# Flags spread over the partitions by a matmul, ranks computed later, and a last output half stored in two pieces

## Chip, cores and metric

One NeuronCore of a Trainium2 chip runs the whole program. The metric is device time in microseconds (us); three plain runs of the kernel before gave 236.74, 237.10 and 233.53 us (median 236.74). One more execution was profiled; its own time was 234.33 us, and its span, from the first to the last instruction, 232.5 us.

## What is computed

The reference is an attention followed by a two-layer network. Four batches of eight heads, 768 positions, head size 64. Each head has a flag: a flagged ("retrieval") head attends to every earlier position, the others to four sink positions and a window of 64. The attention's output, regrouped to 3072 tokens of 512, goes through `h = x @ w_in` (512 to 2048), `g = h - tanh(h)` and `g @ w_out` (2048 to 512).

```python
causal = rel >= 0
stream_keep = causal & (is_sink | in_win)
mask = np.where(is_retrieval[head], causal, stream_keep)
scores = np.where(mask, scale * (q @ k.T), -1e9)
a = softmax(scores)                       # per head
x = (a @ v).transpose(0, 2, 1, 3).reshape(4 * 768, 512)
h = x @ w_in
out = (h - np.tanh(h)) @ w_out            # float32, 3072 x 512
```

The flags are eight 64-bit integers, that is sixteen 32-bit words, in DRAM.

## The kernel before

The 3072 tokens are worked off in twelve tiles `t` of 256 tokens, three to a batch. For each tile the stages are: load q, k, v; turn them so that the head size lies on the partitions (`st_T` on TensorE for tiles 0 to 2, a transposing DMA in `turn` from tile 3 on); scores (`st_S`, line 987) and their exponential on ScalarE (line 1000); the product with v (`st_A`, line 1080), which VectorE divides by the row sums (lines 1100, 1112, 1127); x turned (`st_X`, lines 1161 and 873, for tiles 0 and 1, a transposing DMA in `st_X_tile`, line 1144, from tile 2 on); the first layer in eight units of 256 columns (`H_unit`: eight matmuls at line 1190 into `ph`, tanh on ScalarE at line 1202, the difference on VectorE at line 1209 into `gt`); and the second layer (`O_group`: matmuls at line 1248 into `po`, then `store`, lines 1222 to 1234).

All operations are recorded first (`op`, `dma`) and then put in order by `Plan.run`, which plays them through with estimated costs and writes out each engine's queue in that order. Every engine then works its queue off strictly in order, so a change of one recorded operation, its cost or its dependences can move instructions on all five engines. `Plan.run` also hands out the PSUM banks: the tag `one` has four, and `tp`, `av`, `xp`, `ph` and `po` all live in them, so TensorE has to wait for the reader of a bank before it fills it anew. Spare time of TensorE before 18 us of the planned time is filled with matmuls of `ones` (line 1392, `wm`).

The parts that matter here:

- `flags` (line 717) turns the sixteen words, which line 1308 has loaded into all 128 partitions, into one flag per head (`nz`, `rflag`) and a threshold (`thr`); `masks` (line 746) makes from it the additive masks `m4` of tiles 0 and 1, and `scale_v` multiplies v by it.
- `by_rank` (line 758) sorts the heads, flagged ones first: some fifteen small VectorE operations that end in `perm_i` (line 814), masks `m4r` and `mS` for tiles 3 and up, and two register loads of the ranks (line 863), one on GpSimd's queue, which then gathers the heads by rank (`gather`, line 560), and one on VectorE's.
- GpSimd's queue issues the loads of v for the first tiles (line 434), of q and k for tiles 1 and 2 (`t16p`, line 467), of the weights (`win`, line 539; `wout`, line 550) and of tile 3 (line 528). SyncE's queue issues the loads of tiles 4 and up (line 528), the transposing DMAs (lines 492 and 1144) and the stores (line 1234). `t16p` is copied on VectorE (line 478) before `st_T` of tiles 1 and 2.
- The last token block's output is projected in two halves of 256 columns at the end (lines 1463 and 1464): the first is copied out of PSUM by VectorE and stored by SyncE's queue, the second by ScalarE and ScalarE's queue. Each `store` takes an `ot` buffer of its own.

Of the kernel before, what the change touches and what calls it, by code (L numbers as in the profile page):

```python
# [7 lines left out]
FP32 = mybir.dt.float32  # L8
FP16 = mybir.dt.float16
I32 = mybir.dt.int32  # L10
# [6 lines left out]
class Plan:  # L17
# [24 lines left out]
    def op(self, eng, ns, fn, r=(), w=(), dma=None, prio=None, port=False):  # L42
        i = len(self.ops)
        deps = set()
        for k in r:
            if k in self.writer:
                deps.add(self.writer[k])
            if k[0] in self.PSUM:
                deps.update(j for j in self.readers.get(k, ()) if self.ops[j][0] != eng)
            self.readers.setdefault(k, []).append(i)  # L50
        for k in w:
            if k in self.writer:
                deps.add(self.writer[k])
# [12 lines left out]
        return i  # L66
# [154 lines left out]
def kernel(  # L221
# [49 lines left out]
    engs = {"ACT": nc.scalar, "DVE": nc.vector, "POOL": nc.gpsimd, "SP": nc.sync}  # L271
    Engine = mybir.EngineType

    retr_i = const.tile([128, 2 * H], I32, name="retr_i")
    ones = const.tile([128, 128], FP16, name="ones")
    warm = const.tile([128, 1], FP32, name="warm")
    ident16 = const.tile([128, 128], FP16, name="ident16")
    A4 = const.tile([128, 4, 128], FP16, name="A4")
    sinks = const.tile([128, 128], FP16, name="sinks")
    nz = const.tile([128, 2 * H], FP32, name="nz")  # L280
    rflag = const.tile([128, H], FP32, name="rflag")
    thr = const.tile([128, H], FP32, name="thr")
    m4 = const.tile([128, H, 512], FP16, name="m4")
    rflag0 = const.tile([128, H], FP32, name="rflag0")
    nzp = nz[:].rearrange("p (h two) -> p h two", two=2)
    m4r = const.tile([128, NGEN, 512], FP16, name="m4r")
    rflagr = const.tile([128, NGEN], FP32, name="rflagr")
    rflagr0 = const.tile([128, NGEN], FP32, name="rflagr0")
# [19 lines left out]
        ot=([128, DM], FP32), v1=([128, 2 * NG, H, D + 1], FP16), vf=([128, 4, H, D + 1], FP16),  # L308
    )
    many = []  # L310
    TE = (("ACT", "ACT"), ("DVE", "DVE"), ("DVE", "DVE"))
    SV = "POOL"
    FILLS = 30
    FILL_END = 18000.0
    CASTS = (("ACT", "ACT"), ("ACT", "DVE"))
    CUT = (-10.5, -6.0, 2.25, 13.5)
    GATE = {3: (1, 0), 4: (1, 1)}
    CUT1 = (-10.5, -6.0, 2.25, 13.5)
    FROM = 3
    BR = 8  # L320
    MASKS = 2
    A2 = (10, 14)
    ORDER = (0, 1, 2, 3, 4, 5, "t2", "r3", 6, 7)

    def program(first):
# [18 lines left out]
        def buf(tag):  # L344

            i = rot[tag] = rot.get(tag, -1) + 1
            box = []

            def get():
                if not box:  # L350
                    shp, dt = shape[tag]
                    at = P.bank_of[tag, i] if tag in P.BANKS else i % bufs[tag]
                    box.append(pools[tag].tile(shp, dt, tag=f"{tag}{at}", name=f"{tag}_{i}"))
                return box[0]

            return get, i
# [358 lines left out]
                select(mS[0:64, 3, :], ones[0:64, :], 0.0, n_sink_i - 1, 0, -1, "mS3")  # L715

        def flags():
            op(
                "DVE", 175,
                lambda: nc.vector.tensor_scalar(  # L720
                    out=nz[:], in0=retr_i[:], scalar1=0, scalar2=None, op0=ALU.not_equal
                ),
                r=["retr"], w=["nz"],
            )
            op(
                "DVE", 165,
                lambda: nc.vector.tensor_max(out=rflag[:], in0=nzp[:, :, 0], in1=nzp[:, :, 1]),
                r=["nz"], w=["rflag"],
            )
            op(  # L730
                "DVE", 165,
                lambda: nc.vector.tensor_scalar(
                    out=thr[:], in0=rflag[:], scalar1=-0.5, scalar2=0.75, op0=ALU.mult, op1=ALU.add
                ),
                r=["rflag"], w=["thr"],
            )
            op(
                "DVE", 165,
                lambda: nc.vector.scalar_tensor_tensor(
                    out=rflag0[:], in0=sinks[:, 0:1].to_broadcast([128, H]), scalar=0.75,  # L740
                    in1=rflag[:], op0=ALU.is_ge, op1=ALU.max,
                ),
                r=["sinks", "rflag"], w=["rflag0"],
            )
# [13 lines left out]
        def by_rank():  # L758

            def dve(ns, fn, r, w):  # L760
                op("DVE", ns, fn, r=r, w=w)

            one = iota[:].unsqueeze(1).to_broadcast([128, H, H])
            dve(
# [404 lines left out]
            )  # L1169


        gts, pos, chain = {}, {}, []
        FU = 2
        NFU = NFB // FU

# [38 lines left out]
            )  # L1214

        def store(t, ts, po, key, c0, c1, eng, ring):
            ot, io = buf("ot")
            t0 = t * TT + ts * 128

            def evac():  # L1220
                if eng == "ACT":
                    nc.scalar.activation(  # L1222
                        out=ot()[:, c0:c1], in_=po()[:, c0:c1], func=AF.Copy, scale=1.0 / XS
                    )
                else:
                    nc.vector.tensor_scalar(
                        out=ot()[:, c0:c1], in0=po()[:, c0:c1], scalar1=1.0 / XS, scalar2=None,
                        op0=ALU.mult,
                    )

            op(eng, 110 + 0.95 * (c1 - c0), evac, r=[key], w=[("ot", io), ("od",) + key])
            dma(
                ring, 420,
                lambda: engs[ring].dma_start(out=out[t0 : t0 + 128, c0:c1], in_=ot()[:, c0:c1]),
                128, (c1 - c0) * 0.18, r=[("ot", io)],
            )

        def O_group(t, ts, f0, f1, c0=0, c1=DM, eng="ACT", ring="SP"):

            if f0 == 0:  # L1240
                pos[t] = bank([128, DM], FP32, "one", f"po{t}_{ts}_{c0}")
            po, key = pos[t]
            gt, ig = gts[t]
            for fa in range(f0, f1, 2):

                def mm(fa=fa):
                    for f in range(fa, fa + 2):
                        nc.tensor.matmul(  # L1248
                            out=po()[:, c0:c1], lhsT=gt()[:, f, ts * 128 : ts * 128 + 128],
                            rhs=w_out_t[:, f, c0:c1], start=(f == 0), stop=(f == NFB - 1),  # L1250
                        )

                halves = range(c0 * 2 // DM, (c1 * 2 - 1) // DM + 1)
                if fa == 0:
                    chain.append(key)
                op(
                    "PE", 2 * 0.422 * (c1 - c0), mm,
                    r=[("wout", x, fa * 2 // NFB) for x in halves] + [("gt", ig, fa // FU)]
                    + [("od",) + c for c in chain[-3:-2] if fa == 0], w=[key],
                )  # L1260
            if f1 == NFB:
                store(t, ts, po, key, c0, c1, eng, ring)
# [42 lines left out]
        if first:  # L1305
            dma(
                "ACT", 400,
                lambda: nc.scalar.dma_start(
                    out=retr_i[:], in_=is_retrieval.bitcast(I32).partition_broadcast(128)
                ),  # L1310
                128, 20.0, w=["retr"],
            )
            load_first()
            constants()
            iq = raws[0][1]
            for half in range(2):
# [24 lines left out]
        else:  # L1341
            for t in range(3):
                load_cast(t)
            for n in range(HP):
                st_T(n, TE)
                st_S([(n, 0)])
# [114 lines left out]
            op("SP", 500, count, r=["count", ("gt", gts[last][1], NFU - 1)])  # L1461
        O_group(last, 0, 0, NFB)
        O_group(last, 1, 0, NFB, 0, half, "DVE", "SP")
        O_group(last, 1, 0, NFB, half, DM, "ACT", "ACT")

        with tc.manual_schedule():
            P.run()
# [40 lines left out]
```

## Time and profile before

| | |
|---|---|
| runs | 236.74, 237.10, 233.53 us, median 236.74 |
| profiled execution | 234.33 us, span 232.5 us |
| TensorE clock granted | 0.998 of full speed over the span |
| TensorE matmul busy | 223.0 us (96%), 2345 matmuls |
| VectorE, ScalarE, GpSimd busy | 145.2, 142.9, 100.1 us |
| DMA | 35.3 MB, mean 152 GB/s over the span |

A profile row gives start and duration in us, the engine, the line, what is written and read, and how often; in brackets the idle time of the engine just before it and what ended it. PE is TensorE's matmuls, PEld its weight loads, DVE is VectorE, ACT ScalarE, POOL GpSimd, SP SyncE; a name with q is a queue that issues. Matmuls overlap, so a row of n matmuls lasts n spacings plus the fill of the last. A transfer's landing is the moment at which its semaphore lets a waiter go on; the trace has it for each.

### The profile page before, as it was taken

The page shows a single profiled execution, that of the slowest core. Times are in us where ns is not written, and L with a number is a line of the kernel's source. Part 1 is how long each engine was busy: PE and PEld are TensorE (multiplying, and loading weights), DVE is VectorE, ACT ScalarE, POOL GpSimd, SP SyncE. Part 2 cuts the span into 40 slices and gives each one's busy share as a digit, 9 for nine tenths or more (in the row PEclk, how much of TensorE's full clock was granted, in tenths as well). Part 3 has the DMA queues.
Part 4 walks back from the last instruction along what each step waited for, and adds up shares of the span by engine and source line. Part 5 has one row for each costly group of instructions (what it writes and reads, how often), then busy time and mean ns, then how long its engine had stood idle before and what let it go on. Part 6 is the DMA issues. An engine that isn't in the chain of part 4 may idle for free. (4 is left out here: it accounts for less than half of the span.)

```text
span 232.5 us, 6139 instructions
## 1 busy us (share of the span) xinstructions
PE 223.0 (96%) x2345; PEld 159.5 (69%) x2345; DVE 145.2 (62%) x345; ACT 142.9 (61%) x223; POOL 100.1 (43%) x231
## 2 busy tenths in 40 slices
PE   7888999999999999998999999999999999999992
PEld 7546798888986767656766666667676667666652
DVE  3789668976774967777585465668674465534310
ACT  2867768976466868664855857466835946443320
POOL 8998352990283729467461959291000000000000
PEclk9999999999999999999999999999999999999999
DMA  4999999978999999979999999945103011301112
GB/s 122 195 193 206 197 199 223 209 114 212 245 208 233 163 233 168 244 171 215 187 210 227 227 185 243 230 114 119 39 30 85 15 38 45 93 12 38 45 61 81
DMA packets 103105, 35.31 MB, mean 152 GB/s; under 512 B 90784, under 2 KB 100256, under 8 KB 103072
## 3 DMA queue, kind: packets, MB, share of 16 engines
q1 hardware_dynamic: 85632, 27.14, 57.4%
q0 software_dynamic: 17152, 7.60, 25.0%
q8 instruction: 19, 0.31, 0.6%
q10 hardware_dynamic: 288, 0.14, 0.2%
q14 instruction: 14, 0.11, 0.2%
HBM read 27.27 MB, written 6.29 MB: 144 GB/s over the span
## 5 line engine op out<-in xcount | busy, mean ns | idle before, releaser
L1190 PE MATMUL ph<-xT,win 128*128 128x256 f16 x768 | 99.0, 273 | 1.0 <-DVE gt L1209 0.9
L1248 PE MATMUL po<-wout,gt 128*128 128x512 f16 (+1 forms) x464 | 97.6, 342 | 0.2 <-DVE gt L1209 0.2
L1209 DVE SCALAR_TENSOR_TENSOR gt<-th,ph 128x512 f16<-128x512 f32 x96 | 65.2, 683 | 38.8 <-ACT th L1202 38.3
L1202 ACT ACTIVATE th<-ph 128x512 f32<-128x512 f32 x96 | 57.4, 600 | 51.0 <-PE ph L1190 50.9
L1190 PEld LDWEIGHTS <-win 128*128 128x128 f16 x768 | 71.2, 98 | 18.6 <-DVE gt L1209 1.3
L1000 ACT ACTIVATE pt<-sc 128x768 f16<-128x768 f32 (+1 forms) x60 | 53.1, 918 | 13.7 <-PE sc L987 13.5
L1248 PEld LDWEIGHTS <-gt 128*128 128x128 f16 x464 | 43.1, 98 | 22.8 <-issue 0.4
L572 POOL CAST t<-rawqk 128x256 f16 x72 | 29.1, 451 | 36.5 <-DMA rawqk<-in_k_dram 23.5
L1112 DVE TENSOR_TENSOR x16t<-av,rinv 128x128 f32 (+1 forms) x80 | 22.9, 288 | 1.9
L1222 ACT ACTIVATE ot<-po 128x512 f32<-128x512 f32 (+1 forms) x28 | 14.9, 532 | 14.1 <-PE po L1248 9.1
L987 PE MATMUL sc<-QK 64*128 64x128 f16 (+1 forms) x364 | 22.2, 239 | 1.2 <-DVE QK L875 0.9
L1080 PEld LDWEIGHTS <-pt 128*128 128x128 f16 x420 | 17.1, 97 | 5.9 <-PE sc L987 1.1
L987 PEld LDWEIGHTS <-QK 64*128 64x128 f16 x364 | 12.6, 94 | 12.2 <-issue 8.2
L1023 DVE TENSOR_TENSOR ptn<-ptn,mS 128x512 f16<-128x512 f16 x24 | 12.3, 551 | 13.3 <-ACT ptn L1000 13.3
L608 POOL CAST v<-rawv 128x128 f16 x72 | 20.2, 328 | 0.0
L1000 ACT ACTIVATE ptn<-sc 128x1024 f16<-128x1024 f32 (+1 forms) x18 | 17.1, 952 | 1.1 <-PE sc L987 1.1
L1080 PE MATMUL av<-v,pt 128*128 128x65 f16 x220 | 17.5, 193 | 0.2
L1051 DVE TENSOR_TENSOR pt<-pt,m4r 128x1024 f16<-128x1024 f16 (+1 forms) x18 | 12.1, 672 | 6.4 <-ACT pt L1000 6.4
L1080 PE MATMUL av<-vf,pt 128*128 128x65 f16 x200 | 13.8, 193 | 0.9 <-DVE gt L1209 0.9
L1100 DVE RECIPROCAL rinv<-av 128x4 f32<-128x4 f32 x48 | 8.3, 176 | 7.1 <-PE av L1080 6.9
L1080 PEld LDWEIGHTS <-ptn 128*128 128x128 f16 x132 | 7.4, 97 | 4.1
L1392 PE MATMUL wm<-ones 128*128 128x128 f16 x69 | 7.0, 281 | 1.4 <-POOL ones L670 1.4
(76 smaller groups left out, 139.1 us busy)
## 6 DMA issues: line engine op xcount, KB each, us to landing
out_dram<-ot SPq DMA_DIRECT2D x19, 256.0 KB, 2.5
rawqk<-in_q_dram SPq DMA_DIRECT2D x18, 256.0 KB, 4.8
rawqk<-in_k_dram SPq DMA_DIRECT2D x18, 256.0 KB, 4.8
rawv<-in_v_dram SPq DMA_DIRECT2D x16, 256.0 KB, 5.2
win<-in_moe_w_in_dram POOLq DMA_DIRECT2D x4, 512.0 KB, 10.7
wout<-in_moe_w_out_dram POOLq DMA_DIRECT2D x4, 512.0 KB, 14.1
out_dram<-ot SPq DMA_DIRECT2D x9, 128.0 KB, 3.7
v<-in_v_dram POOLq DMA_DIRECT2D x6, 128.0 KB, 6.4
```

Of the source, the lines that this page charges most:

```text
L572: nc.gpsimd.tensor_copy(out=c5()[:, :, :, s_ : s_ + 1, :], in_=r5()[:, :, :, at, :])
L608: nc.gpsimd.tensor_copy(out=v1s[b]()[:, g * NB : g * NB + NB, RANK[s_] : RANK[s_] + 1, 0:D], in_=rv()[:, :, at, :],)
L987: nc.tensor.matmul(out=sc()[:, hh, o : o + nb * 128], lhsT=lhsT, rhs=QK[p_, hp, q_0 : q_0 + nb * 128], start=not added, stop=not added or ...
L1000: lambda pt=pt, sc=sc, gi=gi, wid=wid: nc.scalar.activation(out=pt()[:, :, 512 * gi : 512 * gi + wid], in_=sc()[:, :, 0:wid], func=AF.Exp, ...
L1023: nc.vector.tensor_mul(out=pv, in0=pv, in1=m[:, 384:640].unsqueeze(1).to_broadcast([128, 2, 256]),)
L1080: nc.tensor.matmul(out=av()[:, i, hh, :], lhsT=pt()[:, hh, co : co + 128], rhs=vv, start=(jb == first_jb), stop=(jb == qb),)
L1112: nc.vector.tensor_mul(out=xt()[:, :, at, :], in0=av()[:, :, hh : hh + 1, 0:D], in1=rinv()[:, :, hh : hh + 1].unsqueeze(3).to_broadcast([1 ...
L1190: nc.tensor.matmul(out=ph()[:, j, :], lhsT=w_in_t[fb // 4][:, cb, f0 : f0 + 128], rhs=xT()[:, :, cb, :], start=(cb == 0), stop=(cb == HP - 1),
L1202: lambda: nc.scalar.activation(out=th()[:], in_=ph()[:], func=AF.Tanh, scale=1.0 / XS),
L1209: lambda: nc.vector.scalar_tensor_tensor(out=gt()[:, u * FU : (u + 1) * FU, :], in0=th()[:], scalar=-XS, in1=ph()[:], op0=ALU.mult, op1=AL ...
L1222: nc.scalar.activation(out=ot()[:, c0:c1], in_=po()[:, c0:c1], func=AF.Copy, scale=1.0 / XS)
L1248: nc.tensor.matmul(out=po()[:, c0:c1], lhsT=gt()[:, f, ts * 128 : ts * 128 + 128], rhs=w_out_t[:, f, c0:c1], start=(f == 0), stop=(f == NF ...
```

## The change

Four edits.

1. The flags are loaded into one partition (sixteen words, one packet) instead of 128. VectorE clears a 128-row tile `nz16` and writes the sixteen non-zero tests into its first row; a matmul with `ones` adds the rows up, which puts the sixteen values on all 128 partitions in a PSUM bank `flags`; a VectorE reduction of each pair by maximum gives `rflag`.
2. Every VectorE operation recorded by `dve` in `by_rank` also reads `("x16", 4)`, the divided output of tile 1's first head pair (`x16_4`), so the planner puts the ranks behind it.
3. The last column half is projected in two pieces of 128 columns: the first goes through VectorE and SyncE's queue, the second through ScalarE and its queue.
4. All three pieces of that block share one `ot` buffer.

```diff
-    retr_i = const.tile([128, 2 * H], I32, name="retr_i")
+    retr_i = const.tile([1, 2 * H], I32, name="retr_i")
+    nz16 = const.tile([128, 2 * H], FP16, name="nz16")
...
+    LATE = [("x16", 4)]
...
         def flags():
+            all_p, key = bank([128, H, 2], FP32, "one", "flags")
+            op("DVE", 100, lambda: nc.vector.memset(nz16[:], 0.0), w=["nz"])
             op(
                 "DVE", 175,
                 lambda: nc.vector.tensor_scalar(
-                    out=nz[:], in0=retr_i[:], scalar1=0, scalar2=None, op0=ALU.not_equal
+                    out=nz16[0:1, :], in0=retr_i[:], scalar1=0, scalar2=None, op0=ALU.not_equal
                 ),
                 r=["retr"], w=["nz"],
             )
+            def mm():
+                nc.tensor.matmul(
+                    out=all_p()[:].rearrange("p h two -> p (h two)"), lhsT=ones[:], rhs=nz16[:],
+                    start=True, stop=True,
+                )
+
+            op("PE", 100, mm, r=["ones", "nz"], w=[key])
             op(
                 "DVE", 165,
-                lambda: nc.vector.tensor_max(out=rflag[:], in0=nzp[:, :, 0], in1=nzp[:, :, 1]),
-                r=["nz"], w=["rflag"],
+                lambda: nc.vector.tensor_reduce(
+                    out=rflag[:], in_=all_p()[:], op=ALU.max, axis=mybir.AxisListType.X
+                ),
+                r=[key], w=["rflag"],
             )
...
             def dve(ns, fn, r, w):
-                op("DVE", ns, fn, r=r, w=w)
+                op("DVE", ns, fn, r=r + LATE, w=w)
...
         def store(t, ts, po, key, c0, c1, eng, ring):
-            ot, io = buf("ot")
             t0 = t * TT + ts * 128
+            later = c0 > 0 and t == NTT - 1
+            if not later:
+                ots[0] = buf("ot")
+            ot, io = ots[0]
+            held = [("ot", io)] if later else []
+            mine = [("piece", io, c0)] if later else [("ot", io)]
...
-                    out=retr_i[:], in_=is_retrieval.bitcast(I32).partition_broadcast(128)
+                    out=retr_i[:], in_=is_retrieval.bitcast(I32).partition_broadcast(1)
                 ),
-                128, 20.0, w=["retr"],
+                1, 20.0, w=["retr"],
...
         O_group(last, 1, 0, NFB, 0, half, "DVE", "SP")
-        O_group(last, 1, 0, NFB, half, DM, "ACT", "ACT")
+        O_group(last, 1, 0, NFB, half, DM - 128, "DVE", "SP")
+        O_group(last, 1, 0, NFB, DM - 128, DM, "ACT", "ACT")
```

The order that `Plan.run` writes out changes with it. On GpSimd's queue one load of v (tile 2) now stands ahead of the q load of tile 2, and two `vf` products (line 661) stand between that q load and the k load; the register load of the ranks stands behind three of tile 3's loads instead of one. On VectorE's queue the ten first rank operations stand behind `x16_4` and ahead of `gt` of unit 2, and the rest is spread between there and `gt` of unit 4. On SyncE's queue the transposing DMA of tile 2's x stands behind two more raw loads, and that of tile 3's x behind two raw loads and the two turning DMAs of tile 4. From about 23 us to the middle of the run the units of TensorE, ScalarE and VectorE, and the transfers of SyncE, stand in a somewhat different order; behind that the queues are the same up to the last block.

More of the change, by code (lines that the diff above doesn't have):

```diff
@@ L279 @@
     sinks = const.tile([128, 128], FP16, name="sinks")
-    nz = const.tile([128, 2 * H], FP32, name="nz")
     rflag = const.tile([128, H], FP32, name="rflag")
@@ L284 @@
     rflag0 = const.tile([128, H], FP32, name="rflag0")
-    nzp = nz[:].rearrange("p (h two) -> p h two", two=2)
     m4r = const.tile([128, NGEN, 512], FP16, name="m4r")
@@ L310 @@
     many = []
-    TE = (("ACT", "ACT"), ("DVE", "DVE"), ("DVE", "DVE"))
+    TE = (("ACT","ACT"),("DVE","DVE"),("DVE","DVE"))
     SV = "POOL"
@@ L314 @@
     FILL_END = 18000.0
-    CASTS = (("ACT", "ACT"), ("ACT", "DVE"))
+    CASTS = (("ACT","ACT"),("ACT","DVE"))
     CUT = (-10.5, -6.0, 2.25, 13.5)
@@ L1169, in st_X @@
             )
-        gts, pos, chain = {}, {}, []
+        gts, pos, ots, chain = {}, {}, {}, []
         FU = 2
@@ L1229, in evac @@
                     )
-            op(eng, 110 + 0.95 * (c1 - c0), evac, r=[key], w=[("ot", io), ("od",) + key])
+            op(eng, 110 + 0.95 * (c1 - c0), evac, r=[key] + held, w=mine + [("od",) + key])
             dma(
@@ L1234, in store @@
                 lambda: engs[ring].dma_start(out=out[t0 : t0 + 128, c0:c1], in_=ot()[:, c0:c1]),
-                128, (c1 - c0) * 0.18, r=[("ot", io)],
+                128, (c1 - c0) * 0.18, r=held + mine,
             )
```

## Prediction

> **What bounds the kernel now.** I read the page's first two parts, then busy time by stretches, the timeline of the first 60 us and of the end, and the landing of each transfer.
>
> ```profile
> span 232.5 us, 6139 instructions
> PE   7888999999999999998999999999999999999992
> DMA  4999999978999999979999999945103011301112
> 6.60:17.70 11.10, 9.03 (x116) 5.38 (x116) 8.83 (x27) 8.10 (x19) 11.10 (x14) 1.00 1.75 186
> 17.70:22.40 4.70, 3.75 (x41) 2.63 (x40) 4.70 (x13) 3.80 (x6) 4.27 (x5) 1.00 1.25 207
> 22.40:60.00 37.60, 37.60 (x513) 31.33 (x513) 28.84 (x71) 28.55 (x46) 18.12 (x33) 1.00 1.21 194
> ```
>
> In the stretches the first number behind the comma is TensorE's busy time. From 22.4 to 60 us it never stops, and from 60 to 215 us it lacks 1.1 us. So TensorE's queue sets the time: what is gained or lost ahead of 22 us, every new stall behind it, and the end, are all that counts. DMA is as busy until about 150 us. The gaps ahead of 22 us:
>
> ```profile
> 5.07 0.17 DVE L720 TENSOR_SCALAR nz<-retr_i 128x16 f32<-128x16 int32 x1 [0.77 <-DMA retr_i<-in_is_retrieval_dram]
> 5.48 0.39 DVE L732 TENSOR_SCALAR thr<-rflag 128x8 f32<-128x8 f32 x1
> 15.41 0.97 DVE L821 TENSOR_SCALAR rflagr<-iota,cnt 128x4 f32<-128x4 f32 x1
> 17.20 0.56 PE L987 MATMUL sc<-QK 64*128 64x256 f16 x10 [0.90 <-DVE QK L875]
> 19.89 0.33 PEld L1190 LDWEIGHTS <-win 128*128 128x128 f16 x4 [0.34 <-DMA win<-in_moe_w_in_dram]
> 20.11 1.14 DVE L841 TENSOR_SCALAR m4r<-A,thrr 128x512 f16<-128x512 f16 x1
> 22.32 0.19 PE L1080 MATMUL av<-vf,pt 128*128 128x65 f16 x1 [0.89 <-DVE gt L1209]
> ```
>
> Twice TensorE waits for a VectorE that is busy with ranks: from 16.1 to 17.20 for tile 1's turned q and k (1.06 us lost), from 21.3 to 22.32 for `gt` of unit 0, which holds the bank that `av` needs (1.05 us). Rank rows that take 0.15 to 0.35 us elsewhere take 0.97 and 1.14 here; they end when GpSimd's row beside them does. Between the two gaps TensorE waits for the second slice of `w_in`, landed at 19.85.
>
> **Flags.** The 128 packets of 64 B of the old load start at 1.92 and land at 5.05; one packet should land by about 3. The row test (0.17), the matmul behind 34 fills of 0.107 us (1.36 + 3.6 = 5.0) and the reduction (0.2) give `rflag` at 5.4, as before at 5.45. Then `thr` waits anyway: its row, like the two behind it, ends at 5.87, with GpSimd's issue row. Masks start at 5.9 as before; their first user is the score matmul at 8.31, behind two ScalarE copies that wait for raw k. Should the packet come later, 13 fills and the first turn (6.6) queue behind the matmul, so it has 1.6 us to spare. So 0. The transport: 128 packets of 8 ns on 16 engines are 0.06 us, but the first raw packet comes only at 2.57, 0.65 behind the old load's first. Later weights come in the same stream, so between 0 and -0.6; I take -0.2.
>
> **Ranks, and what follows on VectorE.** Without them the copies of tile 1's q and k end at 16.15 instead of 17.1; the score matmuls then run from 16.25. But the first slice of `w_in` lands at 17.34 and the second at 19.85, so unit 2's first half still starts at 19.9: the first gap buys nothing. The second goes: `gt` of unit 0 runs at 19.4, and `av4` starts at 21.4 instead of 22.3 (-0.95). `x16_4` then ends at 22.6, and ten rank rows follow, 0.06 to 0.2 apart as at 5.07, 5.28, 5.48: 1.4 us, to 24.0. Behind them queue `gt` of unit 2 (0.69), a mask row (0.35), `gt` of unit 3 (0.69), the reciprocal (0.18), a rank row and a mask row (0.55), and only then `x16_5` (0.43): 26.9, if no row meets a GpSimd row, up to 28.3 if the mask rows do (GpSimd issues at 25.2 and 27.9). In the new order the turn `xp5` stands ahead of unit 6, so TensorE, which is there at 26.4, waits until 27.0 to 28.3 (before, `xp5` ran at 27.8). The lead of 0.95 is down to 0.8, or gone. Then `ph` of unit 7 needs the bank that `gt` of unit 4 frees, now behind two more mask rows and the perm row (28.9 to 29.6): 0.1 to 0.2 lost.
>
> **GpSimd's queue.** One load of v now goes ahead of tile 2's q and k:
>
> ```profile
> 16.13 0.90 POOL L467 DMA_DIRECT2D t16p<-in_k_dram  x1
> 33.22 0.43 DVE L478 COPY t<-t16p 128x1024 f16<-128x1024 f16 x1
> 34.37 0.61 PE L892 MATMUL tp<-ident,t 128*128 128x128 f16 x8
> 34.80 1.44 DVE L875 COPY QK<-tp 128x256 f16<-128x256 f16 x4 [1.15 <-PE tp L892]
> ```
>
> The queue lands in order, and the page's 17.1 us from this k load's issue to landing are its place in the line (33.20); v behind it lands at 34.27. Moved back by one load, k lands at 34.2 (34.0 with the 0.2). The copy used it at once, and TensorE came to the turn 0.7 us later. Now both copies stand on VectorE ahead of the reciprocal and `x16_7`, which complete tile 1's x. So: k 34.2, copy to 34.65, reciprocal and `x16_7` to 35.3, two QK copies to 36.05, scores 36.1 to 36.6, then unit 0 of tile 1 to 37.5. TensorE, early or not, waits here. Before, it had done the same work less four `po` matmuls (0.44) at 36.3. So 37.5 - 0.44 - 36.3 = +0.75, with the ranks' variants between +0.3 and +1.3. The 0.95 is given back, and more. The register load of the ranks is covered: GpSimd waits for a weight landing at 30.25 before its next issue in any case; VectorE's own hid in a wait of 0.6 us and now stands behind `gt` of unit 4.
>
> **SyncE's queue.**
>
> ```profile
> 56.44 1.83 SPq L1144 DMA_TRANSPOSE xT<-x16t  x1
> 58.32 0.57 SPq L528 DMA_DIRECT2D rawqk<-in_k_dram  x1
> 58.94 0.57 SPq L528 DMA_DIRECT2D rawv<-in_v_dram  x1
> 60.76 7.15 PE L1190 MATMUL ph<-xT,win 128*128 128x256 f16 x64
> ```
>
> The first row turns tile 2's x; it lands at 60.25, and its matmuls start at 60.66: 0.4 to spare. The two loads behind it land at 62.09 and 62.91; now they are ahead, and x lands at 62.5 to 62.9. TensorE arrives at 60.7 + 0.65 (six more `po` matmuls stand ahead of it) + 0.55 = 61.9, so 0.6 to 1.0 is lost. Tile 3's x (66.56, 1.7 to spare) moves back to about 71; its unit is behind more work and arrives at 71.6. Tile 4's turned q and k had 0.5 to spare and come 0.9 earlier. I take +0.8, from 0 (loads reach the engines earlier, since SyncE no longer waits for x ahead of them) to +2.5.
>
> **The end.**
>
> ```profile
> 220.46 7.97 PE L1248 MATMUL po<-wout,gt 128*128 128x512 f16 x52
> 228.52 0.38 ACT L1222 ACTIVATE ot<-po 128x256 f32<-128x256 f32 x1 [2.95 <-PEq L1471]
> 228.94 0.36 ACTq L1234 DMA_DIRECT2D out_dram<-ot  x1
> ```
>
> Sixteen matmuls of 256 columns (0.109 each, 1.74) become 32 of 128. The turns above do eight in 0.61 with 0.22 of fill: 0.056 each, 1.79, so +0.05. The copy of 128 columns is 0.27 (512 take 0.60, 256 take 0.38): -0.11. The store (1.7 to landing) has half the bytes: -0.15, between 0 and -0.2. The middle piece, out by 228.1 on VectorE, lands ahead of the last. No piece waits for another's store, since they touch different columns. Together -0.2; bounds -0.3 and, if the weight load (98 ns mean) could not hide, +1.3.
>
> The Trainium skill's "TensorE: Matmul & The Clock Gate", section "Back-to-back issue gap", speaks against this split: in a stream of weight load and matmul, 128 columns sustain about 81 ns each. By that the piece would take 2.6 us and the end be 0.65 us worse instead of 0.2 better. The rows above, with new weights for each matmul, show 56, so the sum doesn't use it.
>
> **Sum.** 0 - 0.2 + 0.75 + 0.8 - 0.2 = +1.15, bounds -0.6 and +5.1. The later stalls (1.6 us between 104 and 146) are left as they are; another order of units may move them either way, to -2.2 in all if they went. Against the profiled 234.33 us that is 235.5. This execution lies 2.4 below the median of the runs; the four executions known spread from 233.5 to 237.1, mean 235.4, and so I give 235.4 + 1.15 = 236.6.
>
> **Rivals.**
> - The gaps stay closed: both VectorE gaps go (-2.1), the stream comes 0.2 earlier, the end gains 0.2, and nothing is given back: 234.33 - 2.5 = 231.8, or 232.9 against the mean. For it: VectorE is busy only 28.8 of 37.6 us from 22.4 on. Against: `w_in` at 19.85, tile 2's k at 34.2. 20%.
> - The transposing DMAs come too late, slower: price 2.7 us for tile 2's x (62.91 - 60.25) less 0.4, 4.5 for tile 3's less 1.7, with no delay of TensorE's own to cover it: +5.1, with +0.75 -0.4 about 239.8, or 240.9 against the mean. It decides once tile 2's x lands behind 61.9. For it: the small slack, DMA 90% busy there. Against: the raw loads start earlier. 16%.
> - Nothing happens: the flags end with GpSimd's row, and the ranks move from one wait to another of the same size: 234.1 to 234.6, 235.4 against the mean. For it: every gap ahead of 22 us lies beside a landing. Against: the order at 34 us. 20%.
>
> **Numbers.** My forecast, a small loss, has 40%; 4% are left for others. Two per cent (4.7 us) is about what a measurement of this kernel can tell from no change. Faster than 232.0 takes the first rival with luck: 5%. Slower than 241.5 needs half of the second, or two of the terms at their upper bounds: 15%. Within: 80%. Range 232.9 to 240.0, the first rival's time to just short of the second's.
>
> **What would show it.** Right: no gap ahead of `av4`; TensorE waiting for `x16_5` near 27 and for the `t16p` copy or the turned tile 2 at 34 to 36; unit 0 of tile 2 waiting for its x near 62; the last 32 matmuls in 1.8 us. Wrong: tile 2's k landed by 33.3, or TensorE at unit 0 of tile 1 before 35.5 (gain), or several waits of over 1 us for transposing DMAs (loss), or a clock that rises later than 6.2 us (where the fills' spacing now halves) because the flag matmul waits in TensorE's queue.

## Result, and the profile after

The changed kernel takes 236.05 us (median of 21 runs, 235.46 to 237.23); the kernel before, measured beside it, 234.54 (21 runs, 233.38 to 238.09). The ratio is 1.0075, with a 95% interval from 1.0053 to 1.0096: a small loss, where 1.15 us (0.5%) had been forecast. Medians here take in every execution, and the kernel before has some of 237 to 239 us; the ratios leave the disturbed ones out, so a ratio can differ from the quotient of two medians.

The profiled execution of the changed kernel took 237.07 us (span 235.3), one of its longest; that of the kernel before (234.33) lies near its median. So of the 2.7 us between the two traces about 1.2 belong to these two executions and not to the kernels. The page after, its span and three rows of slices:

```profile
span 235.3 us, 6188 instructions
PE   7859999999999988999999999999999999999992
PEclk9979999999999999999999999999999999999998
DMA  5999999959999799999999998681212111301112
```

TensorE now has slices below 9 behind 80 us (the two 8s), and its granted clock a 7 in the third slice. Busy times by stretches, the first number behind the comma being TensorE's, the third from the end its clock:

```profile
6.60:22.40 15.80, 12.76 (x144) 8.22 (x141) 10.99 (x28) 10.09 (x21) 14.99 (x18) 0.89 1.52 178
22.40:40.00 17.60, 17.03 (x215) 13.65 (x210) 13.12 (x44) 12.96 (x23) 7.29 (x9) 1.00 1.46 209
40.00:95.00 55.00, 52.96 (x654) 41.01 (x653) 38.91 (x90) 39.13 (x58) 31.48 (x83) 1.00 1.03 192
95.00:150.00 55.00, 54.66 (x561) 36.91 (x560) 34.80 (x82) 34.85 (x52) 34.72 (x90) 1.00 1.09 223
```

The same view of before gives TensorE 12.78, 17.60, 55.00 and 53.91 us: nothing was lost between 22.4 and 95 us, now 2.6 us are, and 0.75 come back behind 95. From the timeline, first the start:

```profile
13.24 1.12 POOL L661 TENSOR_TENSOR vf<-v,rflag 128x520 f16<-128x520 f16 x1
13.32 1.34 DVE L478 COPY t<-t16p 128x1024 f16<-128x1024 f16 x1 [0.67 <-DMA t16p<-in_k_dram]
15.26 1.06 PE L1173 MATMUL xp<-ident,x 128*128 128x128 f16 x6 [2.34 <-DVE x L1139]
```

(Lines 1173, 1202, 1251 and 1265 are the lines 1161, 1190, 1234 and 1248 of before.) The copy of tile 1's k, 0.53 us before, takes 1.34: it starts 0.08 us behind GpSimd's product and ends 0.3 us behind that product's end. In VectorE's queue it stands ahead of the reciprocals and x rows of tile 0, as it did before, and TensorE waits 2.3 us for x. This gap is new; the one ahead of `av4` is gone.

Then the places behind 30 us. Rows of TensorE, with what ended the wait, and the row of SyncE that goes with them:

```profile
35.33 0.51 PE L904 MATMUL tp<-ident,t 128*128 128x128 f16 x6 [0.39 <-DVE t L478]
36.56 0.56 PE L999 MATMUL sc<-QK 64*128 64x256 f16 x10 [0.17 <-DVE QK L887]
63.30 0.94 PE L1202 MATMUL ph<-xT,win 128*128 128x256 f16 x7 [0.49 <-ACT ot L1239]
79.80 2.61 SPq L492 DMA_TRANSPOSE QK<-t  x2
84.39 0.56 PE L999 MATMUL sc<-QK 64*128 64x256 f16 x10 [0.73 <-DMA QK<-t]
91.60 0.61 PE L1202 MATMUL ph<-xT,win 128*128 128x256 f16 x4 [0.82 <-DMA xT<-x16t]
```

The first two are tile 2's k (landed 34.83, before 33.20); the third is tile 2's x, whose transposing DMA landed at 63.25 (the row names ScalarE there, but `ot` is no input of that matmul). The last two had not been forecast: the turned q and k of tile 5 (issued 79.80 instead of 76.98, landed 84.35 instead of 82.44) and tile 4's x. The latter had nothing to spare before either: its DMA landed at 89.28, and the unit that reads it started at once:

```profile
89.33 0.61 PE L1190 MATMUL ph<-xT,win 128*128 128x256 f16 x4
```

The end:

```profile
229.30 0.42 DVE L1243 TENSOR_SCALAR ot<-po 128x256 f32<-128x256 f32 x1 [4.75 <-PE po L1265]
231.09 0.28 ACT L1239 ACTIVATE ot<-po 128x128 f32<-128x128 f32 x1 [2.94 <-PE po L1265]
231.39 0.39 ACTq L1251 DMA_DIRECT2D out_dram<-ot  x1
```

From VectorE's copy of the first 256 columns to the end of the span it is 6.04 us, before 5.78. The last store lands 2.17 us behind its issue, before 1.73.

### The profile page after: what moved, and what is told of

It is laid out like the page before. It is cut to its first block, busy times and chain, and to the rows that moved or that the text cites. A ratio compares the mean times of both kernels' runs of the same rounds, so it can differ in the third digit from the quotient of the medians.

```text
span 235.3 us, 6188 instructions
## 1 busy us (share of the span) xinstructions
PE 223.7 (95%) x2365; PEld 160.2 (68%) x2365; DVE 142.8 (61%) x347; ACT 143.1 (61%) x223; POOL 98.7 (42%) x231
## 4 chain that ended last, share of the span: by engine, by line
PE 72%; DMA 15%; POOL 4%; DVE 4%; SPq 1%; issue 1%; ACT 1%; POOLq 0%; ACTq 0%; DVEq 0%
PE po L1265 31%; PE ph L1202 30%; DMA t16p<-in_k_dram 9%; PE sc L999 6%; PE av L1092 5%; DMA xT<-x16t 2%; DMA rawqk<-in_q_dram 2%; DMA QK<-t 1%; POOL vf L661 1%; POOL v L434 1%; DVE x L1139 1%; DVE t L478 1%; POOL t L572 1%; POOL t16p L467 1%; DVE gt L1221 1%
## 5 line engine op out<-in xcount | busy, mean ns | idle before, releaser
L1265 PE MATMUL po<-wout,gt 128*128 128x512 f16 (+2 forms) x480 | 97.9, 337 | 0.3 <-DVE gt L1221 0.3
L1221 DVE SCALAR_TENSOR_TENSOR gt<-th,ph 128x512 f16<-128x512 f32 x96 | 65.2, 682 | 37.9 <-ACT th L1214 37.7
L1265 PEld LDWEIGHTS <-gt 128*128 128x128 f16 x480 | 43.2, 98 | 22.5 <-issue 0.5
L1239 ACT ACTIVATE ot<-po 128x512 f32<-128x512 f32 (+2 forms) x28 | 14.8, 529 | 14.9 <-PE po L1265 14.9
L608 POOL CAST v<-rawv 128x128 f16 x72 | 19.3, 314 | 0.0
L1035 DVE TENSOR_TENSOR ptn<-ptn,mS 128x512 f16<-128x512 f16 x24 | 10.4, 473 | 13.9 <-ACT ptn L1012 13.9
L1063 DVE TENSOR_TENSOR pt<-pt,m4r 128x1024 f16<-128x1024 f16 (+1 forms) x18 | 12.8, 713 | 6.6 <-ACT pt L1012 6.6
L597 POOL COPY kc<-QK 128x128 f16<-128x128 f16 x12 | 4.1, 341 | 11.0 <-DMA QK<-t 10.9
```

What stands on the lines that cost most here:

```text
L608: nc.gpsimd.tensor_copy(out=v1s[b]()[:, g * NB : g * NB + NB, RANK[s_] : RANK[s_] + 1, 0:D], in_=rv()[:, :, at, :],)
L1063: nc.vector.tensor_mul(out=pv, in0=pv, in1=m)
L1221: lambda: nc.vector.scalar_tensor_tensor(out=gt()[:, u * FU : (u + 1) * FU, :], in0=th()[:], scalar=-XS, in1=ph()[:], op0=ALU.mult, op1=AL ...
L1239: nc.scalar.activation(out=ot()[:, c0:c1], in_=po()[:, c0:c1], func=AF.Copy, scale=1.0 / XS)
L1265: nc.tensor.matmul(out=po()[:, c0:c1], lhsT=gt()[:, f, ts * 128 : ts * 128 + 128], rhs=w_out_t[:, f, c0:c1], start=(f == 0), stop=(f == NF ...
```

## Experiments

Each runs beside the kernel before on one chip, which gave medians of 235.86, 235.60 and 235.52 us in the three groups (29 to 35 runs each, 233.9 to 239.3). "Lost" below is counted from the trace: the spacings of TensorE's matmul starts less what these matmuls take at full clock (0.107 us for 256 columns).

### The parts one by one

Flags alone (edit 1 of the change):

```diff
-    retr_i = const.tile([128, 2 * H], I32, name="retr_i")
+    retr_i = const.tile([1, 2 * H], I32, name="retr_i")
...
+            op("PE", 100, mm, r=["ones", "nz"], w=[key])
```

> The kernel before with the flags' part alone: one packet, the matmul that spreads it, the reduction. Theory: most of what changed ahead of 40 us comes with this part. The first tile's raw q and k land 1.4 to 2.0 us earlier than before (by 7.3 instead of 8.7 us), GpSimd's queue takes one load of v ahead of tile 2's q and k, and tile 2's k lands behind 34.0 instead of 33.2; the time is 0.7 to 1.5 us above the kernel before (ratio 1.003 to 1.006). Whether the k copy of tile 1 on VectorE again takes 1.3 us instead of 0.5 is open: if it does, TensorE waits over 2 us for the first turn of x near 13 us. Rival: the flags cost nothing (within 0.3 us of before), and the ranks carry the loss.

Measured: 234.62 us (233.0 to 238.34), ratio 0.9955 (0.9908 to 1.0001). The landings came as expected (raw k at 6.97, tile 2's k at 34.50), the time did not: no loss shows for this part alone. The copy of k took 0.52. SyncE's queue is reordered too, yet TensorE has no wait over 0.2 us behind 28 us.

Ranks alone (edit 2):

```diff
+    LATE = [("x16", 4)]
...
-                op("DVE", ns, fn, r=r, w=w)
+                op("DVE", ns, fn, r=r + LATE, w=w)
```

> The kernel before with the ranks alone put behind tile 1's first x. Theory: raw q and k land as before (8.7 us), GpSimd's queue is as before ahead of 22 us and tile 2's k lands at 33.2; the gap ahead of av4 near 21 us (1.05 us) goes, and the time lies between 0.8 us below the kernel before and 0.2 above (ratio 0.9966 to 1.001). Rival: the ranks' rows, now behind 22 us, cost the loss: 0.8 us or more above the kernel before.

Measured: 235.33 us (234.45 to 235.83), ratio 0.9980 (0.9943 to 1.0017). As the theory had it: landings as before, the `av4` gap gone; `w_in` (0.70 and 0.52) and two `gt` waits (0.70 at 33, 0.94 at 44) take what was gained. The executions lie within 1.4 us of each other.

The split alone (edits 3 and 4):

```diff
-        O_group(last, 1, 0, NFB, half, DM, "ACT", "ACT")
+        O_group(last, 1, 0, NFB, half, DM - 128, "DVE", "SP")
+        O_group(last, 1, 0, NFB, DM - 128, DM, "ACT", "ACT")
```

> The kernel before with its last column half alone in two pieces of 128 columns; ahead of the last matmuls every queue has the same order as before. As predicted: 0.2 us less. Rival, from the profile of the changed kernel: the last 32 matmuls take 1.8 us, but the last store takes 2.2 us to land instead of 1.7, beside the middle piece's store; from the start of VectorE's copy of the first 256 columns to the end of the span 6.05 us instead of 5.77, so 0.2 to 0.4 us more (ratio 1.001 to 1.002).

Measured: 234.71 us, ratio 0.9988 (0.9936 to 1.0040), too wide for 0.3 us; the profile decides. From VectorE's copy to the end it is 6.27 us, against 5.78, 5.81 and 5.79 in three kernels without the split. The last store took 2.39 to land. The rival holds.

Two pieces, 384 and 128:

```diff
-        O_group(last, 1, 0, NFB, 0, half, "DVE", "SP")
-        O_group(last, 1, 0, NFB, half, DM, "ACT", "ACT")
+        O_group(last, 1, 0, NFB, 0, DM - 128, "DVE", "SP")
+        O_group(last, 1, 0, NFB, DM - 128, DM, "ACT", "ACT")
```

> The kernel before with its last 512 columns still in two pieces, but of 384 and 128 columns instead of 256 and 256: no third store. If the third store is what takes back the gain of the narrow last piece, the last store lands 1.5 to 1.7 us behind its issue here, the last copy takes 0.27 instead of 0.38, and the time is 0.1 to 0.3 us below the kernel before. If the narrow piece itself costs (its matmuls, or a store of 512 bytes a row), the end is 0.1 to 0.3 us longer, as with three pieces.

Measured: 235.57 us, ratio 0.9977 (0.9931 to 1.0023). The last store takes 2.22 us without a third store, but another store was issued 0.66 ahead of it. So this didn't tell narrow rows from company; the next one does.

The split without its middle store (so 128 columns of the last block are missing from the output; one execution):

```diff
-                lambda: engs[ring].dma_start(...),
+                lambda: (later and ring == "SP") or engs[ring].dma_start(...),
```

> The kernel before with its last column half in two pieces, and the store of the middle 128 columns left out. Beside a middle store the last store took 2.2 to 2.4 us from issue to landing, against 1.73 for 256 columns without one. If the company of the middle store is what costs, the last store lands within 1.6 to 1.8 us here; if the narrow rows themselves cost (512 bytes each), it takes 2.1 us or more again.

Measured: the last store lands 1.67 us behind its issue, and from VectorE's copy to the end it is 5.61 us. So rows of 512 bytes are not slow. A store issued 0.7 to 0.9 us ahead is what costs: it takes the 0.17 us that the narrow piece is worth, and more. In the seven kernels with the whole split that stretch is 5.84 to 6.28 us.

The run with pieces of 384 and 128 had a second use. Its queues ahead of the last block are those of the kernel before, and its trace shows what the first gap of TensorE can grow to in that order:

```profile
17.17 2.10 POOL L661 TENSOR_TENSOR vf<-v,rflag 128x520 f16<-128x520 f16 x2
17.21 2.09 DVE L787 TENSOR_TENSOR pos_a<-cnt,pos_b 128x8 f32<-128x8 f32 x1
20.05 0.93 PE L987 MATMUL sc<-QK 64*128 64x256 f16 x10 [3.59 <-DVE QK L875]
```

A rank row of eight columns, 0.15 us in the trace of before, lasts 2.09 beside two GpSimd products. The copies of tile 1's turned q and k stand behind it, and TensorE waits 3.6 us where the trace of before showed 0.9. Little can decide it: in the kernel with the split alone, whose queues are the same there, that row started 0.02 us behind the first product instead of 0.04 and took 0.15. In the kernels that put the ranks behind tile 0's x the wait is at most 0.6 us.

### The changed kernel, one thing at a time

The copy of k moved behind three x rows. The order list of `Plan.run` is edited by hand; operation 58 is that copy, 100 the third x row, 67 the q load of tile 2:

```diff
+        for i, j in self.moves:
+            order.remove(i)
+            order.insert(order.index(j) + 1, i)
...
+            P.moves = ((58, 100), (67, 58))
```

> The changed kernel with one VectorE instruction moved: the copy of tile 1's k stands behind the first three reciprocals and x rows of tile 0 instead of ahead of them; every other queue has the same order. Theory: TensorE's 2.5 us wait for x near 13 us falls below 0.6 and its clock is not halved behind it; but the first slice of w_in lands only at 18.2, so what reaches the end is 0.4 to 1.0 us (235.0 to 235.7). Rival A: nothing reaches the end (within 0.3 us of 236.05), since w_in and tile 2's k hold TensorE anyway. Rival B: the copy, 1 us later, delays tile 1's turns and scores as much as it was to gain, and the time is 0.5 us or more above 236.05.

Measured: 236.70 us, ratio 1.0059 (1.0024 to 1.0093), which overlaps the changed kernel's own interval. The ratio is lower by 0.0016 (0.4 us) and uncertain by twice that: no gain is shown, which speaks for rival A, but the 0.4 us that the theory asked for at least is not ruled out. The wait for x is gone and the clock stays full behind 5.3 us, but TensorE then waits 1.33 and 0.54 us for the first two slices of `w_in` and 1.04 for tile 2's k. Of the new gap at 13 us and the halved clock behind it, little or nothing arrives at the end. The changed kernel's own runs point the same way: the seven with a mean granted clock of 0.998 or more have a median of 235.94 us, the eleven with 0.992 or less 236.24.

The old load of the flags added again, into a tile that nobody reads:

```diff
+                    nc.scalar.dma_start(
+                        out=spare_i[:], in_=is_retrieval.bitcast(I32).partition_broadcast(128)
+                    ),
```

> The changed kernel with the old 128-packet load of the flags issued as well, behind the one-packet load, into a tile that nothing reads; all else is the same. It gives the raw loads of q and k back the company of the old 128 packets. Theory (the stream from GpSimd's queue runs slower because it starts earlier): raw q and k land late again (last one behind 8.3 instead of 7.3 us), tile 1's q and k land at 11.4 and 12.8 again instead of 11.8 and 13.3, the first w_in slice at 17.4 instead of 18.2, and the time is 0.3 to 1.0 us below 236.05 although one load more is made. Rival (that delay is of another source): raw q and k land late, tile 1's k behind 13.1 all the same, and the time is 236.0 or more.

Measured: 236.77 us, ratio 1.0061 (1.0020 to 1.0101). Neither theory whole: the last raw k lands at 7.69, between the two (7.28 and 8.69), the first `w_in` slice at 17.50 as in the kernel before (17.34), but tile 1's k at 13.26 as in the changed one (13.29). With the raws later `w_in` is back near its old time, and no difference to the whole time shows.

Two stretches of queue put back:

```diff
+            P.moves = ((110, 68), (193, 110), (71, 193), (224, 356), (225, 224),
+                       (386, 476), (387, 386), (369, 387), (370, 369))
```

> The changed kernel with two stretches of queue put back by hand: on GpSimd tile 2's q and k go ahead of the load of v again, on SyncE tile 2's and tile 3's transposing loads of x go ahead of the raw k and v loads again; VectorE, TensorE and ScalarE keep the changed kernel's order. Theory (the moved loads carry the loss behind 30 us): tile 2's k lands at 33.8 instead of 34.8; the two waits of TensorE at 34.7 and 36.1 us (0.9 us together) fall to 0.3 or less, the wait for tile 2's x at 62.5 (0.66) goes, and those at 83 and 90 us (1.9 together) shrink; the time is 1.0 to 2.0 us below the changed kernel's 236.05. Rival (the loss sits ahead of 20 us, in the copy of k on VectorE and the later landings of w_in): the time stays within 0.5 us of 236.05, and the waits come back elsewhere.

Measured: 237.76 us, ratio 1.0099 (1.0065 to 1.0134): no faster than the changed kernel's own 1.0075 (the intervals overlap), and the theory is wrong in its sum. Its waits did go (34 to 36 us: 0.5 left; 62, 83 and 90: none), but tile 4's turned q and k, now behind tile 3's x, land at 71.86, and TensorE loses 2.8 us to them. Its granted clock is halved from 71.94 to 75.35, behind that wait, which costs about half of that stretch more (1.7 us). In the changed order TensorE does tile 4's scores ahead of tile 3's units, in the order of before behind the first two of them. The edit had put back SyncE's order and not TensorE's.

Only GpSimd's stretch and tile 2's x put back:

```diff
+            P.moves = ((110, 68), (193, 110), (71, 193), (224, 356), (225, 224))
```

> The changed kernel with GpSimd's tile 2 q and k ahead of the load of v again, and on SyncE tile 2's transposing load of x ahead of the raw k and v loads; the rest of SyncE's queue stays as in the changed kernel. Theory: as with the larger edit, TensorE's waits at 34.7 and 36.1 fall from 0.9 to about 0.5 us and the one at 62.5 (0.66) goes, without the wait of 2.8 us for tile 4's q and k at 71.9; those at 83 and 90 us stay within 0.5 us of 1.9. So 234.6 to 235.4. Rival: what is gained at 36 and 62 is waited for again at 83 and 90 us: within 0.4 us of 236.05.

Measured: 236.59 us, ratio 1.0085 (1.0053 to 1.0117). By the ratios the rival, and earlier than it said. Waits of TensorE between 60 and 95 us:

```profile
PE sc L1005 <- DMA QK<-t: 2.1, 2, 1.7
PE ph L1208 <- DMA xT<-x16t: 0.5, 1, 0.5
```

Of the 0.9 us at 34 to 36, 0.4 are gained, and the 0.66 at 62; but TensorE stands at tile 4's scores from 68.7 to 70.7: that DMA lands at 70.68, in the changed kernel at 70.81, where TensorE had only just come.

The ranks behind tile 0's last x, all else as in the changed kernel:

```diff
-    LATE = [("x16", 4)]
+    LATE = [("x16", 3)]
```

> The changed kernel with one number changed: the ranks stand behind tile 0's last x (x16_3) instead of tile 1's first (x16_4). GpSimd's and SyncE's queues then have the order that the flags' part alone gave them. Theory (the loss comes from the order in which the loads go when both parts meet, and not from a part by itself): the waits of TensorE at 62, 83 and 90 us (2.5 us together in the changed kernel) are gone, and the time is 234.4 to 235.3, at least 0.8 below the changed kernel's 236.05. Rival (each part costs by itself): within 0.4 us of 236.05.

Measured: 234.67 us (234.13 to 236.02), ratio 0.9969 (0.9936 to 1.0002). The theory, with one number changed: all three parts are there, and the loss is gone. GpSimd's queue has the same order as in the changed kernel, so that order is not what carries the loss; SyncE's, TensorE's, VectorE's and ScalarE's differ. TensorE's waits from 60 to 95 us are down to one line:

```profile
PE sc L999 <- DMA QK<-t: 0.5, 1, 0.5
```

Tile 5's turned q and k land at 84.36 here, as late as in the changed kernel (84.35). But TensorE comes to their scores at 85.67 instead of 83.5, with other units in front. The gap ahead of `av4` is back (0.96 us lost at 22.5) and costs nothing that shows.

The same without the split:

```diff
-        O_group(last, 1, 0, NFB, half, DM - 128, "DVE", "SP")
-        O_group(last, 1, 0, NFB, DM - 128, DM, "ACT", "ACT")
+        O_group(last, 1, 0, NFB, half, DM, "ACT", "ACT")
```

> The flags' part and the ranks behind tile 0's last x, without the split of the last column half: the first kernel of this call less that split. By the split's cost in the profile (0.27 to 0.49 us) it is 0.2 to 0.5 us below that kernel, at 234.0 to 235.0, and with the even start of the ranks it beats both the kernel before and the changed one. Rival: the split costs nothing, the two are equal.

Measured: 234.55 us, ratio 0.9964 (0.9933 to 0.9994). From VectorE's copy to the end 5.82 us, against 6.13 in the kernel with the split: 0.3 in the profile, and 0.12 between the medians, which settles nothing by itself.

The ranks alone behind tile 0's last x:

```diff
+    LATE = [("x16", 3)]
...
+                op("DVE", ns, fn, r=r + LATE, w=w)
```

> The kernel before with the ranks alone behind tile 0's last x (x16_3); SyncE's queue has the same order as before, GpSimd's nearly (one register load moves back by one). Theory: the copies of tile 1's turned q and k go ahead of the long rank rows, so the wait of TensorE near 17 us (1.1 to 3.8 us in the runs of before) is at most 0.8 in every execution; the time is 233.8 to 234.9, and the executions lie within 2 us of each other, where those of the kernel before spread over 4 to 5. Rival: the rank rows now hold up gt of unit 0 near 20 us instead, and the time is that of the kernel before with the same spread.

Measured: 234.44 us (234.12 to 235.43), ratio 0.9953 (0.9923 to 0.9983). This beats the kernel before, and by the ratios the changed one by 1.2% (0.9953 / 1.0075 = 0.988). Its executions lie within 1.3 us of each other. The queues of SyncE, GpSimd and ScalarE have the order of before; near 17 us TensorE loses 0.74 instead of 1.06. The profiled execution was its longest (235.43), and it lost time at the two places that the changed kernel loses it, though no transfer was moved:

```profile
83.45 0.56 PE L988 MATMUL sc<-QK 64*128 64x256 f16 x10 [0.39 <-DMA QK<-t]
90.79 0.61 PE L1191 MATMUL ph<-xT,win 128*128 128x256 f16 x4 [0.95 <-DMA xT<-x16t]
```

Tile 5's turned q and k landed at 83.41 here (before 82.44), tile 4's x at 90.74 (89.28). So these two places are tight in the order of before too.

### The account

Lost time of TensorE in the profiled executions, us, from the start of the span (ahead of 22.4 us the matmuls of `ones` count as lost):

| kernel | 0 to 22.4 | 22.4 to 40 | 40 to 95 | 95 to 150 | sum | that execution |
|---|---|---|---|---|---|---|
| before | 12.5 | -0.2 | -0.4 | 1.5 | 13.4 | 234.33 |
| flags alone | 12.0 | 1.9 | -0.7 | 0.0 | 13.1 | 233.98 |
| ranks behind `x16_3` alone | 12.5 | -0.2 | 1.0 | 1.3 | 14.6 | 235.43 |
| all parts, `x16_3` | 11.7 | 2.0 | -0.2 | 0.1 | 13.6 | 234.75 |
| changed (all parts, `x16_4`) | 12.6 | 1.1 | 1.6 | 0.5 | 15.9 | 237.07 |
| changed, k copy moved | 12.2 | 1.3 | 1.3 | 0.5 | 15.2 | 236.26 |
| changed, both loads | 11.8 | 1.3 | 1.7 | 0.7 | 15.6 | 236.66 |
| changed, GpSimd and tile 2's x put back | 12.0 | 0.5 | 2.1 | 0.4 | 15.0 | 236.01 |
| changed, two stretches put back | 12.4 | 0.5 | 3.7 | 0.0 | 16.6 | 237.96 |

(Where scores stand, the count goes below zero: score matmuls on 64 rows run two at a time, ten of 256 columns in 0.56 us.) Time less sum is 220.8 to 221.4 in every line, so the sum is what tells these executions apart. All kernels with the changed kernel's order of TensorE lose 1.3 to 3.7 us between 40 and 95 us, whatever was mended ahead of it. The others lose at most 1.0 there, the 1.0 at the two tight places shown above.

## Why the prediction was right and wrong

The sum forecast a loss, and most waits that it named are there; at +1.15 us it was short of the 1.5 between the medians and the 1.76 of the ratio. Two steps failed: the base on which the sum was set, and the path of the transfers behind the first ones that move on SyncE's queue. The steps, by the two traces:

- **The base.** 1.15 was added to 235.4, a mean over four executions; 21 runs put the kernel before at 234.54, close to the profiled 234.33 that the sum had been made against. As a time, 236.6 is no loss against the median of 236.74 that is given ahead of the prediction, and its bounds of 232.0 and 241.5 are taken from that median: a sum of +1.15 and a time below the stated median do not forecast the same thing. That 236.6 came out near 236.05 is luck: the base was 0.9 too high and the change too small, and the two errors partly cancel.
- **Flags, 0.** Right: `thr` (5.37 to 5.88) still ends with GpSimd's row.
- **Transport, -0.2, between 0 and -0.6.** Mis-sized, and wrong in what follows. Tile 0's last raw k landed 1.4 us earlier (7.28 for 8.69), not 0.2 to 0.6: beside the 128 small packets, which lasted to 5.05, the raw loads had come late all along, and not only until the first packet got through. "Later weights come in the same stream" was wrong: the loads from GpSimd's queue are issued when they were, and then ran slower (9.4 to 12 us: 150 GB/s instead of 176). Tile 1's k landed 0.37 later, the first `w_in` slice 0.84 later. So where 0.2 was to be gained, the weights came later.
- **First gap buys nothing, second gap -0.95.** Both right in kind: the gap ahead of `av4` is gone. But the step missed the copy of k on VectorE: landing later and caught by a GpSimd row, it put tile 0's x 1.2 us back (15.26 for 14.07). Up to 22.4 us TensorE lost 12.6 us, before 12.5. `av4` started at 22.52, not at 21.4: the 0.95 was spent before it was had. The moved copy shows that mending this gap alone would not have helped much: `w_in` and tile 2's k stand behind it. The wait for `x16_5` near 27 us, the right place, was 0.18 us.
- **GpSimd's queue, +0.75 (0.3 to 1.3).** The place and the waits are right: TensorE lost 0.56 us to the copy and 0.34 to the two QK copies. Tile 2's k landed at 34.83, not 34.2, since the whole stream was later. Unit 0 of tile 1 ended at 37.9 instead of 37.5, so the same subtraction gives +1.2 us, within the bounds. But it is no term of a sum: put back, it was waited for again at 70.7, and the kernel with `x16_3` has the same GpSimd queue and no loss.
- **SyncE's queue, +0.8 (0 to 2.5): the term that failed.** Tile 2's x landed at 63.25 (62.5 to 62.9 expected) and cost 0.66; tile 3's x landed at 72.07, its unit started at 72.22, as forecast. The step stopped there. In the changed queue tile 3's x stands behind tile 4's turns and ahead of the next raw loads: raw k is issued at 71.47 instead of 69.75 and lands at 76.10 instead of 73.83. Tile 5's turns and tile 4's x come behind these, and TensorE lost 0.89 and 0.98 us at 84 and 91 us. That the moved x alone does this is not shown: with the ranks behind `x16_3` that raw k lands at 76.06 without the move and nothing is lost there, since TensorE asks later. What the step left out is when each later transfer is asked for; tile 4's x had 0.05 us to spare before (89.28 to 89.33). The rival of late transposing DMAs had this mechanism, at tile 2's and tile 3's x and for 5.1 us; 2.1 were lost between 40 and 95 us, and of the three waits there (0.66, 0.89 and 0.98) three quarters are at tiles 4 and 5.
- **Later stalls, left as they are, to -2.2.** They shrank by 0.9 between 95 and 150 us, within the bound that the text had kept out of its sum.
- **The end, -0.2 (-0.3 to +1.3).** +0.27. The 32 matmuls took 1.79 us (0.056 each, as computed) and the copy 0.28; the store term (-0.15) failed. "No piece waits for another's store" is true, but a store beside another lands later: 2.17 us with one 0.9 ahead, 1.67 without. The Trainium skill's "TensorE: Matmul & The Clock Gate", section "Back-to-back issue gap", has 81 ns a matmul sustained; by that the matmuls would have taken 2.59 us, an estimate from the page's figure, 0.8 more than measured. The trace disagrees. (By its own terms the prediction's end would then have been 0.6 us worse, not 0.65.)

In all, by the same count: +0.10 us ahead of 22.4 us, +1.29 to 40, +2.06 to 95, -0.94 to 150, +0.06 to VectorE's last copy of 256 columns, +0.27 behind it: the 2.84 us between the two spans.

What had not been seen is the larger lesson: the loss is in no part. Flags alone and ranks alone each come out at or below the kernel before; only the two dependences together made the planner put out an order in which TensorE reaches several transposing DMAs before they land. That it is the order, and not the parts, is shown by the run with `x16_3`, whose interval lies clear of the changed kernel's. Which of that order's many differences is enough by itself stays open: two attempts to put back a stretch by hand moved the wait to another DMA. Why the stream from GpSimd's queue runs slower when it starts earlier stays open as well; the run with both loads gave part of it back.

## What to carry to other kernels

When a planner writes the order, cost a small edit by the order that comes out and follow every queue past the first moved transfer, to the transfers behind it and to the moment at which each is asked for; a stall removed in front of a late transfer is only moved to it. Look for the transfers that have no time to spare before the edit. Try the same edit with a neighbouring dependence before judging it: one number here was worth about 1% of the time (ratios 1.0075 and 0.9969). And a long wait of one engine can be a short instruction of another that a third holds up: look for rows that take ten times their usual time.

## What the runs showed of the hardware that was not expected

- TensorE's clock is halved for a stretch of 3.41 us (6.83 in two runs) behind a stretch of 3.41 us in which it was idle enough; one long idle time is not needed. The kernels with the flags alone, where the longest wait was 1.2 us, and with both loads, by windows on the clock's own steps:

```profile
10.95:14.36 3.41, 1.92 (x26) 0.98 (x24) 2.09 (x8) 1.52 (x2) 3.41 (x5) 1.00 1.97 171
14.36:17.77 3.41, 3.37 (x27) 2.26 (x28) 3.41 (x16) 1.45 (x4) 3.00 (x5) 0.50 1.26 206
10.83:14.24 3.41, 2.07 (x29) 1.10 (x28) 1.38 (x7) 1.95 (x4) 3.41 (x5) 1.00 2.00 175
14.24:17.65 3.41, 2.73 (x33) 1.71 (x34) 3.28 (x11) 2.08 (x5) 3.41 (x5) 1.00 1.26 206
```

  Behind 1.92 of 3.41 us busy at full clock comes half clock (0.50), behind 2.07 none. In the changed kernel it was 1.05 of 3.41. In the fourteen traces all six halvings follow stretches with 0.78 to 1.92 us busy, and no stretch at full clock with 2.07 or more was followed by one; one stretch with 1.88, the first behind the clock's rise in the kernel with the split alone, was not either. The Trainium skill's "TensorE: Matmul & The Clock Gate", section "What's actually happening", has the clock fall after at least one idle window of about 3.4 us; the length agrees, but the window here was more than half busy.
- VectorE rows that read and write SBUF can be held by a GpSimd product that runs when they start, and then end 0.03 to 0.33 us behind it: 1.34 instead of 0.43 us for the copy of k, 2.09 instead of 0.15 for a rank row that met two. Not all are: reductions of 0.20 to 0.21 us passed, and the copy of k that started 0.2 us ahead of the product, in the kernel before, took 0.53. Copies out of PSUM were not held: the QK copies beside such products took 0.43 to 0.45 each. This agrees with the Trainium skill's "SBUF — State Buffer", section "SBUF: two separate sides", by which the shared port pair is held for a whole instruction and the loser is blocked.
- A load of 128 packets of 64 bytes, 0.06 us of the DMA engines' time, went with the first four loads of q and k landing 1.2 to 2.1 us later than without it. Issued 0.6 us later, in the run with both loads, it went with the last three landing 0.2 to 1.1 us later than in the changed kernel.
